# Attention with a routed expert layer: the gate work of the first six token pairs spread over nine steps

## The chip, the cores and the metric

The kernel runs on one core of a Trainium2 chip. The metric is the device time of one execution in microseconds (us); before the change it is 973.6 us, the median of three runs (972.81 to 974.79). The engines named below are PE (TensorE, matmuls and transposes), DVE (VectorE), ACT (ScalarE), POOL (GpSimd) and SP (SyncE, which issues DMAs here). PSUM is the memory that PE writes, SBUF the one that all engines share. A row of the timeline gives the start from the span's start, the duration, the engine, the source line, the operation and the tiles, out<-in.

## The reference

Three layers follow one another, on 4 x 576 = 2304 tokens of width 512:

```python
# 1. attention, 8 heads of 64, a causal window of 128 tokens, a bias that falls with distance
scores = scale * q @ k.T ; scores = where(mask, scores + bias, -1e9)
attn = exp(scores - max) ; attn /= sum + 1e-9 ; x = attn @ v
# 2. a routed layer: each token goes to its best two of 8 experts (512 -> 1024 -> 512)
noisy = x @ w_gate + log1p(exp(x @ w_noise)) * noise
top2 = the two largest ; w = softmax over them
out[token] += w * (relu(x[token] @ w1[e]) @ w2[e])
# 3. a dense layer for all tokens (512 -> 2048 -> 512)
out = (relu(x @ w_in) ** 2) @ w_out
```

## The kernel before

The order of the work on each engine is the order in which the program calls the functions; nothing reorders it. Tokens come in 18 tiles of 128 (`NT`), and attention runs in 36 steps (`NV`), two for each tile, four heads to a step. In step v, PE does the scores of step v + 2 (`s_step`, line 257), the transposes of the exponentials of step v + 1 (`t_step`, line 279) and the product with the values of step v (`pv_step`, line 303, called PV below). DVE reduces the scores in four instructions (line 262: add the bias, take the extreme), ACT takes the exponential (268) and copies the transposes out of PSUM (281), and DVE divides by the row sums (`norm`, 314 to 320). The finished tile is stored to `xd` by SP (326).

Beside this, each pair of tiles needs its routing: `gate_t` transposes a tile on PE (333) and ACT copies it (337); `gate_w` (344) and `gate_m` (352) are the two matmuls of the gate, `gate_o` 0 to 4 on DVE (363 to 377) finds the best two experts and makes their one-hot rows `oh`; `rank` (387) counts on PE, with matmuls against a triangle and ones, how many earlier tokens chose the same expert, and updates the running count `acc` (390); `place` 0 to 5 on DVE (397 to 422) turns this into a slot number `pos`; `scatter` on POOL (428) writes the token's number to that slot by two indirect DMAs for each tile. `gate_t`, `gate_w`, `gate_m` and `rank` all write to the one PSUM bank of tag "c".

Where this stands is set by a table: `at(v, slot, f, ...)` puts a call into a slot of step v, and `run(v, slot)` makes the calls of a slot. Slots 0 to 3 are on DVE behind each of the four score reductions, slot 4 stands between the transposes and PV, slot 5 at the step's end behind PV and `norm`:

```python
s_step(v + 2, v)          # slots 0 to 3 are run inside, behind the four reductions
t_step(v + 1)
run(v, 4)
pv_step(v); norm(...)     # and loads of q, k, v; the weight chunk of POOL (prep_one)
run(v, 5)
```

POOL also splits eight chunks of the expert weights in these steps (`prep_one`, line 108 a cast, line 110 a subtraction of 1024 columns), one each fourth step. Three blocks of the first expert's tokens are fetched while attention still runs: `early_table` (501, SP) loads the list of slots once the first 6, 10 or 14 tiles are scattered, `gather` (441, POOL, an indirect DMA) fetches the rows of that list, and `x_in` (448, PE) transposes them. After the last step the experts' matmuls follow, and then the dense layer.

Of the kernel before, what the change touches and what calls it, by code (L numbers as in the profile page):

```python
# [17 lines left out]
OP = mybir.AluOpType  # L18
# [11 lines left out]
PARTS = (6, 10, 14)  # L30
# [19 lines left out]
def attn_moe_ffn(ctx: ExitStack, tc: tile.TileContext, qt, kt, vt, wgn, noise, w1, w2, w_in, w_out,  # L50
                 consts, out):
    nc = tc.nc
# [18 lines left out]
    def bank(tag):  # L71
        if tag == "b":
            return psum.tile([128, 2, 512], F32, name="psb", tag="b", bufs=2)
        return psum.tile([128, 512], F32, name="ps" + tag, tag=tag, bufs={"a": 3, "c": 1}[tag])
# [11 lines left out]
    nload, nprep = [0], [0]  # L86
# [47 lines left out]
    acc = const.tile([128, 2, 8], BF16, name="acc")  # L134
# [17 lines left out]
    def load_q(i):  # L152
        Q[i] = qp.tile([128, 4, 128], F32, name="q", tag="q", bufs=4)
        nc.sync.dma_start(out=Q[i], in_=qt[i])

    def load_k(b, k0=0, k1=S):
        if b:
            K[b] = qp.tile([128, 4, S], F32, name="k", tag="k", bufs=2)
        nc.sync.dma_start(out=K[b][:, :, k0:k1], in_=kt[b][:, :, k0:k1])

    def load_v(n):
        b, p = divmod(n, 5)
        V[n] = qp.tile([128, 2, 8, 65], F32, name="v", tag="v", bufs=5)
        nc.sync.dma_start(out=V[n], in_=vt[b][:, 2 * p:2 * p + 2])
# [55 lines left out]
    P2, PT, PX, XI, G = {}, {}, {}, {}, {}  # L220
# [3 lines left out]
    def at(v, slot, f, *a):  # L224
        todo.setdefault((v, slot), []).append((f, a))

    def run(v, slot):
        for f, a in todo.pop((v, slot), []):
            f(*a)
# [42 lines left out]
    def t_step(v):  # L272
        PT[v] = []
        for j, p2 in enumerate(P2.pop(v)):
            flat = p2.rearrange("p a n -> p (a n)")
            ps = bank("a")[:, :384]
            for m in range(3):
                sl = slice(m * 128, (m + 1) * 128)
                nc.tensor.transpose(ps[:, sl], flat[:, sl], ident)
            pt = wk.tile([128, 3, 128], F32, name="pt", tag="pt", bufs=4)  # L280
            nc.scalar.activation(out=pt, in_=ps.rearrange("p (m c) -> p m c", m=3), func=AF.Copy)
            PT[v].append(pt)

    def pv_step(v):
        i, g = divmod(v, 2)
        px = bank("b")[:, :, :130].rearrange("p a (j d) -> p a j d", j=2)
        PX[i, g] = px
        mms = []
        for part in range(2):
            for j, pt in enumerate(PT[v]):  # L290
                for x in range(2):
                    b, t = divmod(2 * i + x, TB)
                    sl = slice(64 * x, 64 * x + 64)
                    for a in range(2):
                        h = 4 * g + 2 * j + a
                        if part == 0:
                            if a or t:
                                mms.append((x, a, j, pt[:, 2 * a, sl], vs(b, t - 1 + a)[:, h, :]))
                        elif a == 0 or t > 1:
                            r = slice(64 * a, 64 * a + 64)  # L300
                            mms.append((x, a, j, pt[r, 1, sl], vs(b, t - 2 if a else t + 1)[r, h, :]))
        for n, (x, a, j, l, r) in enumerate(mms):
            nc.tensor.matmul(px[64 * x:64 * x + 64, a, j, :], l, r,  # L303
                             start=not any(m[:2] == (x, a) for m in mms[:n]),
                             stop=not any(m[:3] == (x, a, j) for m in mms[n + 1:]), skip_group_check=True)
        del PT[v]
# [72 lines left out]
    def rank(p):  # L379
        oh = G["oh", p]  # L380
        rk = bank("c")[:, 0:16].rearrange("p (q w) -> p q w", q=2)
        G["rk", p] = rk
        for q in range(2):
            terms = [(tri, oh[:, q])] + [(ones, oh[:, 0])] * q + [(ones, acc)]
            for m, (l, r) in enumerate(terms):
                for k in range(2):
                    nc.tensor.matmul(rk[:, q, :], l, r[:, k, :], start=(m + k == 0),
                                     stop=(m + k == len(terms)))
        for q in range(2):
            nc.vector.tensor_tensor(out=acc, in0=acc, in1=oh[:, q], op=OP.add)  # L390

    def place(p, n):
        gs, oh = G["gs", p], G["oh", p]
# [120 lines left out]
    last = NV - 1  # L514
    for p in range(NT // 2):
        v = 4 * p + 3
        end = v == last
        at(v - end, 4, gate_t, 2 * p)
        at(v + 1, 4, gate_t, 2 * p + 1)
        at(v + 2, 0 if end else 4, gate_w, p)  # L520
        at(v + 2, 0 if end else 5, gate_m, p)
        o = v + 2 if end else v + 3
        for n, c in enumerate((0, 0, 0, 1, 2)):
            at(o, c, gate_o, p, n)
        at(o, 4 if end else 5, rank, p)
        for n, c in enumerate((0, 1, 1, 2, 2, 3)):
            at(o + 1, c, place, p, n)
        at(o + 1, 3, scatter, 2 * p)
        if end or 2 * p + 2 == PARTS[-1]:
            at(o + 1, 4, scatter, 2 * p + 1)  # L530
        else:
            at(o + 2, 3, scatter, 2 * p + 1)
    at(3, 3, more_consts)
    at(4, 4, zero_rows)
    for j, (v, w, x) in enumerate(((17, 18, 20), (25, 26, 28), (2 * PARTS[-1] + 3, 2 * PARTS[-1] + 4, last + 1))):
        at(v, 4, early_table, j)
        at(w, 5, gather, 0, j, True)
        at(x, 5, x_in, 0, j)
    at(last, 5, keep_warm, 24)
# [7 lines left out]
    def v_free(n):  # L547
        b, m = divmod(n, 5)
        return 9 * b + min(2 * m + 3, 8)
# [3 lines left out]
    for v in range(-2, NV + 3):  # L553
        s_step(v + 2, v)
        if 0 <= v + 1 < NV:
            t_step(v + 1)
        run(v, 4)
        if 0 <= v < NV:
            i, g = divmod(v, 2)
            pv_step(v)  # L560
            for n in range(3):
                norm(i, g, n)
            if g:
                if nq < NT:
                    load_q(nq)
                    nq += 1
                while nv < 5 * B and v_free(nv - 5) <= 2 * i + 1:
                    load_v(nv)
                    nv += 1
                if nk < B and 2 * i + 1 >= 9 * (nk - 1) + 1:  # L570
                    load_k(nk)
                    nk += 1
            if v % 4 == 2 and nprep[0] < 8:
                prep_one("pool", "pool")
        run(v, 5)

# [32 lines left out]
    for c in range(16):  # L609
        c = 8 * (c % 2) + c // 2  # L610
# [343 lines left out]
    last = E - 1  # L954
# [175 lines left out]
    end = 56 * NSB  # L1130
# [85 lines left out]
    for n, (s, u, kk) in enumerate(batches):  # L1216
# [8 lines left out]
        for k in range(2):  # L1225
            st, en = kk + k == 0, kk == 3 and k == 1
            for m, (p, o, lead) in enumerate(((P1, b13[:, 0:256], True), (P2, b26[:, 0:256], True),
# [9 lines left out]
                if m == 0:  # L1237
                    p1, u3 = tmp[2 + late_][:, 0:256], tmp[late_][:, 0:256]
                    x, y = [rows.tile([128, DM], F32, name="x", tag="r", bufs=6) for _ in range(2)]
# [71 lines left out]
```

## Time and profile before

| | |
|---|---|
| median of three runs | 973.6 us (972.81 to 974.79) |
| the profiled execution, and its span | 974.33 us, 972.6 us |
| PE busy | 956.8 us, 98% of the span |
| DVE, ACT, POOL busy | 69%, 48%, 41% |
| from 0 to 140 us: PE, DVE, ACT, POOL busy | 131.68, 98.93, 99.40, 66.63 us |
| from 140 us to the end: PE busy | 825.17 of 832 us |

Matmuls are pipelined and their ends are modelled, so a stretch of PE is best read from the start of one group to the start of the next. The "[idle <-X]" at the end of a row is idle time of that engine in front of the instruction, and what ended it. Idle time of an engine that is not the bottleneck costs nothing.

### The profile page before, as it was taken

The page shows a single profiled execution, that of the slowest core. Times are in us where ns is not written, and L with a number is a line of the kernel's source. Part 1 is how long each engine was busy: PE and PEld are TensorE (multiplying, and loading weights), DVE is VectorE, ACT ScalarE, POOL GpSimd, SP SyncE. Part 2 cuts the span into 40 slices and gives each one's busy share as a digit, 9 for nine tenths or more (in the row PEclk, how much of TensorE's full clock was granted, in tenths as well). Part 3 has the DMA queues.
Part 4 walks back from the last instruction along what each step waited for, and adds up shares of the span by engine and source line. Part 5 has one row for each costly group of instructions (what it writes and reads, how often), then busy time and mean ns, then how long its engine had stood idle before and what let it go on. Part 6 is the DMA issues. An engine that isn't in the chain of part 4 may idle for free. (4 is left out here: it accounts for less than half of the span.)

```text
span 972.6 us, 19636 instructions
## 1 busy us (share of the span) xinstructions
PE 956.8 (98%) x7438; PEld 878.9 (90%) x7438; DVE 668.2 (69%) x1452; ACT 463.2 (48%) x887; POOL 401.8 (41%) x433
## 2 busy tenths in 40 slices
PE   9999999999999999999999999999999999999997
PEld 6777789898998989899898898999999999999997
DVE  5777754657686776757774436778577899877773
ACT  7778733334343443433343346655555564434341
POOL 1565542124232333415334032624211624888880
PEclk9999999999999999999999999999999999999999
DMA  9767525456667576656655453966537874443331
GB/s 324 283 213 271 176 89 155 143 172 215 204 212 233 165 238 193 236 186 210 203 196 192 149 174 94 300 197 175 163 102 222 234 230 156 152 137 125 130 109 44
DMA packets 118199, 180.00 MB, mean 185 GB/s; under 512 B 11232, under 2 KB 66288, under 8 KB 117712
## 3 DMA queue, kind: packets, MB, share of 16 engines
q1 hardware_dynamic: 107120, 146.77, 46.8%
q0 software_dynamic: 10976, 31.90, 10.5%
q8 instruction: 59, 0.97, 0.4%
q14 instruction: 44, 0.36, 0.1%
HBM read 124.33 MB, written 54.30 MB: 184 GB/s over the span
## 5 line engine op out<-in xcount | busy, mean ns | idle before, releaser
L476 ACT ACTIVATE ha<-psa 128x384 fp32r<-128x384 f32 x64 | 31.3, 491 | 94.8 <-PE psa L472 93.2
L872 POOL TENSOR_TENSOR gs<-xb 128x256 f32<-128x256 f32 x62 | 60.2, 992 | 29.3 <-DVE wc L872 15.4
L268 ACT ACTIVATE p<-p,mx 128x192 f32<-128x192 f32 x144 | 57.5, 450 | 27.4 <-DVE mx L262 26.6
L689 POOL TENSOR_TENSOR et<-ex,et 128x512 f32<-128x512 f32 x16 | 20.9, 1304 | 111.5 <-DVE ex L685 111.5
L710 POOL DMA_INDIRECT yr<-yg,pos x36 | 37.3, 1037 | 68.6 <-DVE ha L477 45.1
L477 DVE SCALAR_TENSOR_TENSOR ha<-psa,ha 128x384 fp32r<-128x384 f32 x64 | 35.4, 553 | 42.6 <-ACT ha L476 37.5
L472 PE MATMUL psa<-xa,wa 128*128 128x384 f32 x288 | 55.0, 343 | 0.0
L428 POOL DMA_INDIRECT slots<-tok,pos x36 | 35.0, 972 | 45.7 <-DVE rs L314 30.0
L886 POOL DMA_DIRECT2D raw<-w x49 | 27.2, 561 | 63.5 <-DVE wb L872 18.4
L441 POOL DMA_INDIRECT xr<-xd,gidx x40 | 44.8, 1119 | 20.9 <-issue 6.1
L472 PE MATMUL psa<-xa,wc 128*128 128x384 f32 x288 | 53.3, 335 | 0.0
L791 PE MATMUL psb<-wa,ha 128*128 128x512 f32 x216 | 52.8, 396 | 0.0
L472 PEld LDWEIGHTS psa<-xa,wa 128*128 128x128 f32 x288 | 51.0, 194 | 0.2
L262 DVE CUSTOM_DVE_ANT_0 p<-psb,bias 128x192 f32<-128x192 f32 x144 | 45.8, 352 | 6.1 <-PE psb L257 5.4
L472 PEld LDWEIGHTS psa<-xa,wc 128*128 128x128 f32 x288 | 49.6, 188 | 0.2
L795 ACT ACTIVATE yo<-psb 128x512 f32<-128x512 f32 x38 | 22.7, 598 | 54.4 <-PE psb L791 38.7
L791 PEld LDWEIGHTS psb<-wa,ha 128*128 128x128 f32 x216 | 39.5, 188 | 7.8
L689 POOL TENSOR_TENSOR ex<-ex 128x512 f32<-128x512 f32 x12 | 15.6, 1302 | 74.6 <-DVE ex L685 74.6
L791 PE MATMUL psb<-wb,ha 128*128 128x512 f32 x176 | 46.3, 397 | 0.0
L110 DVE TENSOR_TENSOR wa<-raw,wa 128x1024 fp32r<-128x1024 f32 x20 | 25.7, 1284 | 29.4 <-ACT wa L106 29.3
L872 DVE TENSOR_TENSOR wc<-gs,wc 128x512 fp32r<-128x512 f32 x48 | 44.4, 965 | 0.4 <-ACT wc L872 0.4
L303 PEld LDWEIGHTS psb<-v,pt 64*64 64x64 f32 (+1 forms) x1056 | 32.8, 135 | 11.0 <-issue 7.7
(330 smaller groups left out, 2726.9 us busy)
## 6 DMA issues: line engine op xcount, KB each, us to landing
raw<-in_w_dram SPq DMA_DIRECT2D x64, 512.0 KB, 4.9
xb<-gmid SPq DMA_DIRECT2D x72, 256.0 KB, 2.9
v<-in_vt_dram SPq DMA_DIRECT2D x20, 520.0 KB, 5.3
yg<-yo SPq DMA_DIRECT2D x40, 256.0 KB, 3.1
raw<-w POOLq DMA_DIRECT2D x36, 256.0 KB, 3.8
gmid<-yo SPq DMA_DIRECT2D x48, 192.0 KB, 3.2
ex<-in_w_in_dram SPq DMA_DIRECT2D x16, 512.0 KB, 4.1
ex<-in_w_out_dram SPq DMA_DIRECT2D x16, 512.0 KB, 3.5
```

The lines of the kernel that those rows point to most:

```text
L262: nc.vector.tensor_tensor_reduce(out=p2[j][:, a, :], in0=ps[:, a, j, :], in1=bias[:, 4 * g + 2 * j + a, :], op0=OP.add, op1=OP.min, scale= ...
L268: nc.scalar.activation(out=p2[j][:, a, :], in_=p2[j][:, a, :], func=AF.Exp, bias=mx[j][:, a:a + 1], scale=-1.0)
L303: nc.tensor.matmul(px[64 * x:64 * x + 64, a, j, :], l, r, start=not any(m[:2] == (x, a) for m in mms[:n]), stop=not any(m[:3] == (x, a, j) ...
L428: st = nc.gpsimd.indirect_dma_start(out=slots, out_offset=bass.IndirectOffsetOnAxis(ap=pos[:, i, k:k + 1], axis=0), in_=tok[:, i:i + 1], i ...
L441: nc.gpsimd.indirect_dma_start(out=XR[e, j], out_offset=None, in_=xd[0:PARTS[j] * 128] if early else xd, in_offset=bass.IndirectOffsetOnAx ...
L472: nc.tensor.matmul(o, w[wp][:, f * 128:(f + 1) * 128], x[:, xp, d, :], start=(n == 0), stop=(n == 11))
L476: nc.scalar.activation(out=hi, in_=ps, func=AF.Relu)
L477: nc.vector.scalar_tensor_tensor(out=lo, in0=ps, scalar=0.0, in1=hi.bitcast(F32), op0=OP.max, op1=OP.subtract)
L689: nc.gpsimd.tensor_tensor(out=x, in0=af, in1=cf, op=OP.add)
L710: nc.gpsimd.indirect_dma_start(out=YR[i, k], out_offset=None, in_=yg, in_offset=bass.IndirectOffsetOnAxis(ap=pos[:, i, k:k + 1], axis=0))
L791: nc.tensor.matmul(py, h[:, hq], wc[wp][:, wsl], start=(f + n == 0), stop=(f == 7 and n == 2))
L872: f(**a)
```

## The change

The table for the pairs 0 to 5 (`2 * p + 2 < PARTS[-1]`) is rewritten; the pairs 6 to 8 keep theirs. With v = 4p + 3, pairs 0 to 4 now have: the two `gate_t` in slot 5 (they were in slot 4) of steps v and v + 1; `gate_w` in slot 4 of v + 2; `gate_m` in slot 4 of v + 3 (it was in slot 5 of v + 2); `gate_o` 0 to 2 in v + 4 and 3 to 4 in v + 5 (all five were in v + 3); `rank` and `place` 0 in slot 5 of v + 6; the update of `acc`, which becomes a function `count`, and `place` 1 to 5 in v + 7 (`place` was in v + 4); the first scatter in v + 7 and the second in v + 9 (they were in v + 4 and v + 5). Pair 5 has all of `gate_o` in v + 4, `rank` and `place` 0 in v + 5, the rest of `place` and the first scatter in v + 6, and the second scatter in v + 7. The early blocks move: tables from steps 17 and 25 to 21 and 28, gathers from 18 and 26 to 22 and 30, `x_in` from 20 and 28 to 24 and 32; the third stays. POOL's weight chunks move from steps 2, 6, 10, ... 30 to 2, 4, 8, 12, ... 28.

```diff
--- before.py
+++ after.py
@@ -386,8 +386,10 @@
                 for k in range(2):
                     nc.tensor.matmul(rk[:, q, :], l, r[:, k, :], start=(m + k == 0),
                                      stop=(m + k == len(terms)))
+
+    def count(p):
         for q in range(2):
-            nc.vector.tensor_tensor(out=acc, in0=acc, in1=oh[:, q], op=OP.add)
+            nc.vector.tensor_tensor(out=acc, in0=acc, in1=G["oh", p][:, q], op=OP.add)
 
     def place(p, n):
         gs, oh = G["gs", p], G["oh", p]
@@ -515,6 +517,26 @@
     for p in range(NT // 2):
         v = 4 * p + 3
         end = v == last
+        if 2 * p + 2 < PARTS[-1]:
+            mid = 2 * p + 4 >= PARTS[-1]
+            at(v, 5, gate_t, 2 * p)
+            at(v + 1, 5, gate_t, 2 * p + 1)
+            at(v + 2, 4, gate_w, p)
+            at(v + 3, 4, gate_m, p)
+            for n, c in enumerate((0, 0, 1, 2, 3) if mid else (0, 0, 1)):
+                at(v + 4, c, gate_o, p, n)
+            if not mid:
+                at(v + 5, 0, gate_o, p, 3)
+                at(v + 5, 1, gate_o, p, 4)
+            o = v + 5 if mid else v + 6
+            at(o, 5, rank, p)
+            at(o, 5, place, p, 0)
+            at(o + 1, 0, count, p)
+            for n, c in enumerate((0, 1, 1, 2, 3)):
+                at(o + 1, c, place, p, n + 1)
+            at(o + 1, 3, scatter, 2 * p)
+            at(o + 2 if mid else o + 3, 3, scatter, 2 * p + 1)
+            continue
         at(v - end, 4, gate_t, 2 * p)
         at(v + 1, 4, gate_t, 2 * p + 1)
         at(v + 2, 0 if end else 4, gate_w, p)
@@ -523,6 +545,7 @@
         for n, c in enumerate((0, 0, 0, 1, 2)):
             at(o, c, gate_o, p, n)
         at(o, 4 if end else 5, rank, p)
+        at(o, 4 if end else 5, count, p)
         for n, c in enumerate((0, 1, 1, 2, 2, 3)):
             at(o + 1, c, place, p, n)
         at(o + 1, 3, scatter, 2 * p)
@@ -532,8 +555,8 @@
             at(o + 2, 3, scatter, 2 * p + 1)
     at(3, 3, more_consts)
     at(4, 4, zero_rows)
-    for j, (v, w, x) in enumerate(((17, 18, 20), (25, 26, 28), (2 * PARTS[-1] + 3, 2 * PARTS[-1] + 4, last + 1))):
-        at(v, 4, early_table, j)
+    for j, (v, w, x) in enumerate(((21, 22, 24), (28, 30, 32), (2 * PARTS[-1] + 3, 2 * PARTS[-1] + 4, last + 1))):
+        at(v, 4 if j == 2 else 5, early_table, j)
         at(w, 5, gather, 0, j, True)
         at(x, 5, x_in, 0, j)
     at(last, 5, keep_warm, 24)
@@ -570,7 +593,7 @@
                 if nk < B and 2 * i + 1 >= 9 * (nk - 1) + 1:
                     load_k(nk)
                     nk += 1
-            if v % 4 == 2 and nprep[0] < 8:
+            if (v == 2 or v and v % 4 == 0) and nprep[0] < 8:
                 prep_one("pool", "pool")
         run(v, 5)
 
```

On PE, a step that ends with a gate transpose (line 333; 257 are scores, 279 transposes of the exponentials, 303 is PV) reads before, in step 19:

```order
L257 MATMUL psb<-k,q 64x192 x8
L279 MATMUL psa<-cst,p_1589 128x128 x3
L279 MATMUL psa<-cst,p_1595 128x128 x3
L333 MATMUL psc<-cst,xi 128x128 x4
L303 MATMUL psb<-v,pt 64x65 x16
```

The same gate transpose after the change, in step 23, with the place work's step 22 in front of it, which now holds the second gate matmul (352):

```order
L257 MATMUL psb<-k,q 64x192 x8
L279 MATMUL psa<-cst,p_1698 128x128 x3
L279 MATMUL psa<-cst,p_1704 128x128 x3
L352 MATMUL psc<-trs,gt 128x16 x2
L303 MATMUL psb<-v,pt 64x65 x16
L257 MATMUL psb<-k,q 64x192 x8
L279 MATMUL psa<-cst,p_1778 128x128 x3
L279 MATMUL psa<-cst,p_1784 128x128 x3
L303 MATMUL psb<-v,pt 64x65 x16
L333 MATMUL psc<-cst,xi 128x128 x4
```

The gate transpose went behind PV, and `gate_m` went between the transposes and PV of a step of its own.

On DVE, the update of the running count (line 390, after the change 392) and the cast that starts the place work (397, 399) stand before, for pair 3 in steps 18 and 19, so (262 is a score reduction, 320 the end of `norm`):

```order
L320 TENSOR_TENSOR xi<-psb,rs 128x256
L390 TENSOR_TENSOR acc<-acc,oh 128x16 x2
L262 ISA p_1589,mx<-psb,bias 128x192
L262 ISA mx 128x1
L397 CAST ri<-psc 128x16
L262 ISA p_1589,mx<-psb,bias 128x192
```

After the change, in steps 21 and 22:

```order
L320 TENSOR_TENSOR xi<-psb,rs 128x256
L399 CAST ri<-psc 128x16
L262 ISA p_1778,mx<-psb,bias 128x192
L262 ISA mx 128x1
L392 TENSOR_TENSOR acc<-acc,oh 128x16 x2
L403 TENSOR_SCALAR ri<-ri 128x16
```

The two additions went from ahead of the first score reduction to behind it, and the cast the other way.

On POOL, around the gather of the first early block (line 441, after the change 443; 428 and 430 are scatters), before:

```order
L108 CAST wb<-raw 128x1024
L110 TENSOR_TENSOR wb<-raw,wb 128x1024
L441 DMA xr<-xd,gidx_109 128x512
L427 MEMSET spacer 1x1
L428 DMA slots<-tok,pos 9728x1
```

And after:

```order
L108 CAST wb<-raw 128x1024
L110 TENSOR_TENSOR wb<-raw,wb 128x1024
L429 MEMSET spacer 1x1
L430 DMA slots<-tok,pos 9728x1
L429 MEMSET spacer 1x1
L430 DMA slots<-tok,pos 9728x1
L443 DMA xr<-xd,gidx_109 128x512
```

The first tile's two scatters of pair 3 went in front of the gather, which stood ahead of them.

## Rows read from the trace of the kernel before

**Rows 1.** Windows, steps 3-10, 11-22, 23-26, 27-32: stretch, length, busy us, clock, DMA share.

```profile
16.36:44.73 28.37, 26.13 (x495) 19.98 (x485) 21.02 (x126) 21.54 (x58) 15.73 (x17) 1.00 0.83 305
44.73:86.55 41.82, 40.36 (x723) 30.73 (x723) 31.69 (x202) 32.79 (x86) 23.81 (x31) 1.00 0.74 260
86.55:100.27 13.72, 13.22 (x247) 10.05 (x247) 10.47 (x66) 10.73 (x29) 7.58 (x9) 1.00 0.60 191
100.27:121.18 20.91, 20.43 (x355) 15.57 (x357) 15.93 (x100) 16.92 (x44) 11.20 (x17) 1.00 0.57 191
```

**Rows 2.** Waits from 8 to 130 us: who waited, for whom, total, times, longest.

```profile
PE psc L387 <- DVE oh L375: 3.1, 5, 1.2
```

**Rows 3.** PE timeline, steps 20 to 24: start, us, operation, tile, out<-in.

```profile
78.88 0.66 PE L448 MATMUL psa<-cst,xr 128*128 128x128 f32 x4
79.47 0.88 PE L257 MATMUL psb<-k,q 64*64 64x192 f32 x16
80.28 0.88 PE L279 MATMUL psa<-cst,p 128*128 128x128 f32 x6
81.08 0.64 PE L344 MATMUL psc<-xt,wg_sb 128*32 128x256 f32 x8
81.65 1.13 PE L303 MATMUL psb<-v,pt 128*64 128x65 f32 x32
82.71 0.62 PE L352 MATMUL psc<-trs,gt 128*128 128x16 f32 x4
83.26 0.88 PE L257 MATMUL psb<-k,q 64*64 64x192 f32 x16
...
86.11 0.20 PE L387 MATMUL psc<-oh,tri 128*128 128x8 bf16 x2
...
86.55 0.88 PE L257 MATMUL psb<-k,q 64*64 64x192 f32 x16
87.36 0.88 PE L279 MATMUL psa<-cst,p 128*128 128x128 f32 x6
88.08 0.63 PE L333 MATMUL psc<-cst,xi 128*128 128x128 f32 x4
88.64 1.13 PE L303 MATMUL psb<-v,pt 128*64 128x65 f32 x32
...
89.81 0.87 PE L257 MATMUL psb<-k,q 64*64 64x192 f32 x16
...
92.12 1.13 PE L303 MATMUL psb<-v,pt 128*64 128x65 f32 x32
93.07 0.33 PE L257 MATMUL psb<-k,q 64*64 64x192 f32 x2
```

**Rows 4.** PE timeline, the score group of step 16.

```profile
61.84 0.65 PE L257 MATMUL psb<-k,q 64*64 64x128 f32 x16
```

**Rows 5.** VectorE timeline, step 23.

```profile
87.06 0.36 DVE L390 TENSOR_TENSOR acc<-acc,oh 128x16 bf16<-128x16 bf16 x2
...
89.39 0.35 DVE L262 CUSTOM_DVE_ANT_0 p<-psb,bias 128x192 f32<-128x192 f32 x1
```

**Rows 6.** GpSimd timeline, step 6.

```profile
28.05 2.35 POOL L110 TENSOR_TENSOR wa<-raw,wa 128x1024 fp32r<-128x1024 f32 x1
```

**Rows 7.** VectorE timeline, step 6.

```profile
29.26 1.19 DVE L375 TENSOR_TENSOR oh<-iota,sel 128x32 bf16<-128x32 uint32 x1
```

**Rows 8.** GpSimd timeline, steps 24 and 25: first of four scatters, then the cast.

```profile
90.10 1.01 POOL L428 DMA_INDIRECT slots<-tok,pos  x1 [5.95 <-DVE rs L314]
...
94.93 1.05 POOL L108 CAST wb<-raw 128x1024 fp32r<-128x1024 f32 x1
```

**Rows 9.** Tile view of xr, all 40 gathers: issue to landing.

```profile
DMA to landing us min/median/max: 3.2/5.1/6.9
```

**Rows 10.** ScalarE timeline, step 20.

```profile
79.19 0.61 ACT L337 ACTIVATE xt<-psc 128x512 f32<-128x512 f32 x1
```

**Rows 11.** DMA view from 60 to 130 us: the table loads.

```profile
gidx<-slots SPq DMA_DIRECT2D x3, 0.5 KB, 2.0
```

## The prediction

> **What bounds the kernel now.** I read the engine table first: PE is busy 98% of the span, so a change counts where PE stands still or does dearer work. The code puts the change into steps 3 to 32 of the attention loop, so I cut that part by the windows view into four stretches whose borders are starts of a step's score group on PE: steps 3 to 10, 11 to 22, 23 to 26 and 27 to 32 [rows 1]. There PE works for 26.1 of 28.4, 40.4 of 41.8, 13.2 of 13.7 and 20.4 of 20.9 us, while VectorE, ScalarE and GpSimd have a fifth or more of their time free, and the granted clock is 1.00. So PE sets the pace and has little to give back. The waits view names its largest stall: the rank matmuls wait 3.1 us in five places for VectorE's one-hot rows [rows 2]. The PE timeline of steps 20 to 24 [rows 3] has the prices, read from start to start, because ends of matmuls are modelled: scores to transposes 0.81 (79.47 to 80.28); transposes to a group with another tile shape 0.80 (80.28 to 81.08), to gate transposes of their own shape 0.72 (87.36 to 88.08); gate transposes to PV 0.56, gate_w to PV 0.57; PV to scores 0.95 (92.12 to 93.07), but PV to a 128-wide group 1.06 (81.65 to 82.71); four transposes in front of scores 0.59 (78.88 to 79.47), gate_m 0.55, ranks 0.44.
>
> **The change, part by part.** One pair before costs four steps: 3.79 (gate_w and gate_m), 3.29 (ranks), 3.26 and 3.26 (gate transposes), 13.60 in all [rows 3].
>
> Gate transposes go from ahead of PV to behind it. PE pays 0.81 + 0.80 + 1.06 + 0.59 = 3.26, against 0.81 + 0.72 + 0.56 + 0.95 = 3.04: dearer by 0.22, twelve times. But before did not run at 3.04: the steps last 3.26, and the first because the next scores (89.81) need the fourth score reduction, started at 89.39 with the place work in between [rows 5]. So these steps stay at 3.26: a stall turns into PE work.
>
> Ranks join gate_w: 0.81 + 0.80 + 0.57 + 1.06 + 0.44 = 3.68, and the one-hot is a step old, so no wait for it. gate_m gets a step with count and places. PE needs only 0.81 + 0.72 + 0.56 + 0.95 = 3.04 there (gate_m to PV taken like gate transposes to PV), but VectorE does not: place work that made 3.26 now also has the two count additions between the reductions, where before they ran ahead of the first one, in idle time; two of 0.18 more [rows 5], one cast less, +0.2: 3.46. A pair: 3.26 + 3.26 + 3.68 + 3.46 = 13.66, as much as before without collisions.
>
> Collisions are what goes. While GpSimd subtracts a chunk (28.05, 2.35 us) [rows 6], VectorE's one-hot comparison at 29.26 takes 1.19 us instead of some 0.19, and ends as the subtraction ends [rows 7]. After the change a subtraction follows four scatters (4.83 from 90.10 to 94.93) and a cast of 1.05 [rows 8], so it starts 6 us behind the first scatter, which comes 0.3 after the following step's scores (90.10 after 89.81): in the gate_w step, where VectorE's gate work reads PSUM.
>
> Steps 3 to 10: two gate steps of 3.26, gate_w alone 0.81 + 0.80 + 0.57 + 0.95 = 3.13, gate_m alone 3.04, then a pair: 26.35 against 28.37, -2.0. The third chunk comes earlier, right behind the second one in GpSimd's order and as soon as its weights land, and its subtraction can hit the first pair's one-hot: between 0 and the 1.0 of rows 7; I take 0.5. Net -1.5.
>
> Steps 11 to 22: three pairs, 40.98, less 0.5 for two narrower score groups (0.65 busy [rows 4] against 0.88), which both kernels have: 40.5 against 41.8, -1.3. Of that 0.7 is a block transpose (0.59 + 0.11) that leaves for step 24.
>
> Steps 23 to 26: a pair, plus that transpose. Behind gate transposes, of its own shape, it costs 0.48 (four of the six that take 0.72): 14.14. Here I add a wait. Step 22 now holds place and scatter of the fourth pair, and on GpSimd two scatters stand in front of the first early gather. They start 0.3 into step 23, take 2.4, so the gather starts at 2.7 and lands 5.1 later [rows 9], at 7.8. PE reaches the transpose at 3.26 + 0.81 + 0.80 + 1.06 + 0.48 = 6.4: it waits 1.4. The scatter must also wait until the table load has read the slots. SP issues that behind a store and two loads of step 21, I estimate 2 us into step 22, and it lands 2.0 later [rows 11], some 0.6 behind the places: wait 2.0, between 0 (gather at its shortest, 3.2, and the table in time) and 4.7 (gather at 6.9, table 1.5 late). Behind it on PE is the whole attention, so it counts in full. 16.1 against 13.7, +2.4.
>
> Steps 27 to 32: the sixth pair is squeezed. Step 27 has all one-hot work, like before's 3.29. In step 28 gate transposes and ranks share the one PSUM bank of that tag, so the ranks wait for ScalarE's copy. In step 20 that copy ended at 79.19 + 0.61 = 79.80 [rows 10], 0.92 after PE was through with PV (78.88): the step costs 0.81 + 0.72 + 0.56 + 1.06 + 0.95 + 0.44 = 4.54, and 4.6 with a little wait of the transposes too; bounds 3.6 (copy early) and 5.0. Then 3.79, 3.29, 3.26 and 3.26 + 0.70 for the second block transpose, now in step 32: 22.2. Its gather stands behind four scatters, starts 4.9 into step 30, lands at 10.0; PE is there at 3.29 + 3.26 + 0.81 + 0.72 + 0.56 + 1.06 = 9.7: 0.3 more (0 to 2.1). 22.5 against 20.9, +1.6.
>
> SP's weight loads, moved with GpSimd's chunks, I cost at nothing: each has four steps until it is used, the load between the first two chunks excepted, which GpSimd waits for in any case. The last three pairs keep their places, and the tail behind attention is PE's, so a shift passes through.
>
> **Sum:** -1.5 - 1.3 + 2.4 + 1.6 = +1.2 us. The profiled execution took 974.33 us (span 972.6), so 975.5 for it; the median of the runs, 973.6, lies 0.7 lower, and on it I forecast 974.8.
>
> **A rule weighed against the rows.** Rows 6 and 7 show a subtraction holding a comparison of two SBUF operands; no such VectorE instruction met GpSimd's cast. The Trainium skill, "SBUF — State Buffer", Who interferes with whom, says that a VectorE instruction with two SBUF inputs contends with any GpSimd instruction that reads SBUF, and that the later one blocks wholly. By that the cast would block too, which no row here shows.
>
> **Rivals.**
> 1. Forecast: the stall of the ranks is paid back by waits for the early gathers and the squeezed pair: 974.8 (own range 973.2 to 975.5).
> 2. Slower: the first early block. If gathers land in 6 us and the table 1.5 late, the first wait is 2.7 + 1.5 + 6.0 - 6.4 = 3.8 and the second 4.9 + 6.0 - 9.7 = 1.2, 2.7 over mine: 977.5. It decides once the first wait is over 2.8. For it: the landings go up to 6.9 [rows 9]. Against: DMA share there is only 0.6 [rows 1].
> 3. Faster: gathers land in 3.2, no wait at all (-2.3), and the third chunk hits nothing (-0.5): 972.0; without the wait for ScalarE in step 28 (-0.95) 971.1. For it: DMA is less busy in the later steps.
> 4. The cast blocks as well: in steps 7 and 8 the third chunk then holds VectorE up to 1.05 longer [rows 8]: 975.8. This is the rule above.
> 5. The change doesn't do what it says: the subtractions drift onto other two-operand work, count or places. Two or three hits of 0.3 to 1.0 cost 1.5: 976.3.
>
> **How the numbers follow.** 0.2% is 1.95 us, about what a measurement of this kernel can tell from no change. Chances: forecast 0.45; rival 2 0.25; rival 3 0.15; rival 4 0.07; rival 5 0.08. Rivals 2, 4 and most of 5 are slower (0.38), rival 3 faster (0.15), the rest within 0.2% (0.47). The range goes from rival 3 at 972.0 to rival 2, 977.4.
>
> **What would show it.** Right: no rank wait for one-hot rows in steps 9 to 25; no VectorE instruction of 0.3 us or more among the small gate ones; gate transpose steps at 3.26, the place steps at 3.4 to 3.5 with scores released by the reduction; PE waiting some 2 us for the DMA of the first early block, and about 1 us for ScalarE in front of the sixth ranks. Wrong: no wait for the block in step 24 (then it is faster), place steps at 3.1, or gate steps over 3.4.

## The result: slower by one per cent

The median after the change is 984.12 us (982.37 to 986.67, 6 runs), against 973.94 us (972.81 to 975.07, 6 runs) before: ratio 1.0100, 95% interval 1.0084 to 1.0115. The forecast, 974.8 us, was wrong, and its range ended at 977.4. The profiled execution took 982.96 us (span 981.1), 8.5 us of span more than before. Two executions of one kernel below (the early block alone: 1150 and 1548 us, at a mean clock of 0.76 and 0.56) were slow ones and are left out of its numbers.

The windows view of the changed kernel, cut at the same score groups as [rows 1] (stretch, length, busy time of PE, PEld, DVE, ACT and POOL with counts, granted clock, DMA share, GB/s):

```profile
17.18:43.49 26.31, 25.64 (x484) 19.62 (x475) 19.42 (x115) 20.84 (x56) 11.49 (x9) 1.00 0.91 340
43.49:86.01 42.52, 39.52 (x719) 30.29 (x719) 33.79 (x201) 32.36 (x85) 22.84 (x30) 1.00 0.73 251
86.01:107.96 21.95, 15.90 (x250) 11.76 (x250) 10.92 (x67) 11.49 (x30) 8.61 (x11) 0.84 0.39 133
107.96:131.61 23.65, 20.81 (x363) 15.89 (x363) 17.07 (x113) 18.12 (x47) 15.04 (x24) 1.00 0.44 145
```

Against [rows 1] that is -2.06, +0.70, +8.23 and +2.74, in sum +9.61. One stretch carries the loss, and its granted clock is 0.84 where the others have 1.00. The attention loop also begins 0.82 later; behind it the kernel is some 1.9 us shorter, mostly because a stretch at the lower clock when the expert work begins, which the profile of before has, is absent in this one.

The waits from 8 to 140 us (who waited, for whom: total, times, longest) answer [rows 2]:

```profile
PE psa L450 <- DMA xr<-xd,gidx: 6.2, 2, 5.8
PE psb L257 <- DVE rs L314: 2.7, 6, 0.6
PE psc L387 <- ACT xt L337: 1.1, 1, 1.1
...
PE psc L387 <- DVE oh L375: 0.2, 1, 0.2
```

The ranks' wait for one-hot rows, 3.1 us before, is gone as predicted; the 0.2 left belongs to a later pair. In its place stands the wait for the first early block, 5.8 us. The PE timeline at that place:

```profile
91.94 0.66 PE L333 MATMUL psc<-cst,xi 128*128 128x128 f32 x4
98.36 1.12 PE L450 MATMUL psa<-cst,xr 128*128 128x128 f32 x4 [5.77 <-DMA xr<-xd,gidx]
99.41 0.42 PE L246 MATMUL psb<-far,ones 64*64 64x256 bf16 x2
99.42 1.54 PE L257 MATMUL psb<-k,q 64*64 64x192 f32 x16
100.89 1.54 PE L279 MATMUL psa<-cst,p 128*128 128x128 f32 x6
```

The same score and transpose groups took 0.87 us each at 89.28 and 90.08. The windows of 2 us say why: the clock is granted at 0.50 (1.2 GHz) when PE resumes.

```profile
94.00:96.00 2.00, 0.00 (x0) 0.00 (x0) 0.00 (x0) 0.00 (x0) 1.78 (x4) 1.00 1.04 396
96.00:98.00 2.00, 0.00 (x0) 0.00 (x0) 0.00 (x0) 0.00 (x0) 1.91 (x2) 0.54 0.22 78
98.00:100.00 2.00, 1.64 (x18) 1.31 (x20) 0.00 (x0) 0.48 (x1) 1.10 (x2) 0.50 0.00 0
100.00:102.00 2.00, 2.00 (x17) 1.41 (x12) 1.65 (x8) 0.68 (x3) 0.00 (x0) 0.50 0.00 0
102.00:104.00 2.00, 2.00 (x33) 0.95 (x34) 0.66 (x3) 1.68 (x5) 0.00 (x0) 0.75 0.00 0
```

Where the block's lateness comes from is read on three engines. On SP (start, duration of the issue), the table load stands behind a store and two loads of step 21:

```profile
83.02 0.34 SPq L326 DMA_DIRECT2D xd<-xi  x1
83.45 1.31 SPq L154 DMA_DIRECT2D q<-in_qt_dram  x1
84.86 0.38 SPq L164 DMA_DIRECT2D v<-in_vt_dram  x1
85.34 0.37 SPq L503 DMA_DIRECT2D gidx<-slots  x1
```

VectorE has the fourth pair's places at 85.94:

```profile
85.78 0.16 DVE L424 TENSOR_TENSOR pos<-gs,cst 128x4 int32<-128x4 f32 x1
```

but GpSimd starts the first scatter only at 89.44, 4.1 us after the table load's issue, because the scatter may not write the slots before the table has been read. The releaser that the view infers (DVE rs) had long been done; that it was the load is shown by the run below that moves the load alone (there the scatter starts at 86.40).

```profile
89.44 0.99 POOL L430 DMA_INDIRECT slots<-tok,pos  x1 [9.11 <-DVE rs L317]
...
92.03 1.00 POOL L443 DMA_INDIRECT xr<-xd,gidx  x1 [0.30 <-issue]
```

The gather stands behind both scatters, and its landing took 6.3 us, with the 16 DMA engines full until 96 us (above, a share of 1.04 in 94 to 96, 0.22 in the next 2 us):

```profile
DMA to landing us min/median/max: 6.3/6.3/6.3
```

In steps 11 to 22 the steps with the second gate transposes took 3.72, 3.52 and 3.72 us. GpSimd and VectorE in the first of them (rows of the kind of [rows 6] and [rows 7]):

```profile
48.59 1.05 POOL L108 CAST wa<-raw 128x1024 fp32r<-128x1024 f32 x1
```

```profile
48.53 1.16 DVE L375 TENSOR_TENSOR oh<-iota,sel 128x32 bf16<-128x32 uint32 x1
```

The comparison, some 0.19 us by itself, ends as the cast ends (49.64). The cast blocks it, not the subtraction, and does so in the third and fourth pair too (1.27 and 1.16 us). In the first pair it is the third chunk's subtraction, which runs from 33.16 to 35.53, that holds the comparison:

```profile
34.61 0.96 DVE L375 TENSOR_TENSOR oh<-iota,sel 128x32 bf16<-128x32 uint32 x1
```

### The profile page after: what moved, and what is told of

It reads as the page before. It is cut to its first block, busy times and chain, and to the rows that moved or that the text cites. A ratio compares the mean times of both kernels' runs of the same rounds, so it can differ in the third digit from the quotient of the medians.

```text
span 981.1 us, 19631 instructions
## 1 busy us (share of the span) xinstructions
PE 956.6 (97%) x7438; PEld 878.5 (90%) x7438; DVE 669.0 (68%) x1452; ACT 463.2 (47%) x887; POOL 399.9 (41%) x433
## 5 line engine op out<-in xcount | busy, mean ns | idle before, releaser
L818 ACT ACTIVATE yo<-psb 128x512 f32<-128x512 f32 x38 | 22.7, 597 | 54.5 <-PE psb L814 40.5
```

## The experiments

Each kernel ran against the kernel before on the same chip (medians there 974.9, 974.3 and 974.5 us). First all of them by stretches, in us, from their profiled executions with the borders of [rows 1]; then the ratio of the times to before.

| kernel | 3-10 | 11-22 | 23-26 | 27-32 | sum | median us | ratio, 95% |
|---|---|---|---|---|---|---|---|
| before | 28.37 | 41.82 | 13.72 | 20.91 | 104.82 | 973.9 | 1 |
| predicted | 26.85 | 40.5 | 16.1 | 22.5 | 105.95 | 974.8 | |
| changed | 26.31 | 42.52 | 21.95 | 23.65 | 114.43 | 984.1 | 1.0084 to 1.0115 |
| block's transposes in step 27 | 26.29 | 42.52 | 14.90 | 25.78 | 109.49 | 980.3 | 1.0039 to 1.0088 |
| table load ahead | 26.17 | 42.56 | 14.11 | 23.23 | 106.07 | 976.7 | 1.0007 to 1.0037 |
| table and gather ahead | 26.46 | 42.56 | 14.94 | 23.33 | 107.29 | 976.7 | 1.0011 to 1.0040 |
| wait filled | 26.46 | 42.55 | 20.00 | 23.82 | 112.83 | 983.4 | 1.0076 to 1.0117 |
| early block alone | 28.75 | 41.36 | 18.68 | 21.00 | 109.79 | 978.7 | 1.0029 to 1.0065 |
| chunks alone | 28.65 | 42.95 | 13.71 | 20.79 | 106.10 | 977.9 | 1.0018 to 1.0047 |
| table ahead, chunks back | 25.93 | 42.15 | 20.44 | 27.57 | 116.09 | 987.8 | 1.0118 to 1.0151 |
| table ahead, one-hot later | 25.93 | 40.57 | 14.33 | 23.88 | 104.71 | 979.2 | 1.0034 to 1.0064 |
| table ahead, sixth ranks | 27.28 | 42.52 | 17.42 | 25.95 | 113.17 | 977.4 | 1.0015 to 1.0041 |
| table ahead, three edits | 25.65 | 39.75 | 18.38 | 23.10 | 106.88 | 977.7 | 1.0015 to 1.0056 |
| three edits, both blocks ahead | 25.65 | 39.76 | 13.65 | 21.99 | 101.05 | 970.6 | 0.9944 to 0.9975 |
| before, chunk between scatters | 27.03 | 42.83 | 15.24 | 20.82 | 105.92 | 974.2 | 0.9982 to 1.0006 |

**The block's transposes moved from step 24 to 27**

```diff
-((21, 22, 24), (28, 30, 32), ...)   # table load, gather, transposes
+((21, 22, 27), (28, 30, 32), ...)
```

> Only the transposes of the first early block move, from step 24 to step 27; its table load, its gather, the scatters and all gate work stay as in the changed kernel. Theory A (the block's wait and the fall of the granted clock behind it are the loss): PE has three more steps, over 10 us, so the wait of 5.77 us is gone, the granted clock stays at 1.00, and the groups at half clock (L450 1.06, scores to transposes 1.47, transposes to gate_w 1.47, gate_w 0.86, together some 2.1 us more than at full clock) are gone too: 984.1 - 5.8 - 2.1 = 976.2 us. Theory B (the spread gate work itself costs, the wait only stands where another stall would): 982 to 984 us, with the idle time on other groups of steps 23 to 28.

Measured 980.33 us: the wait for the block is gone, but of the loss in the median only a little over a third (half of it in the stretches). What takes its place is read in step 26. The late table still makes the scatters late, so GpSimd's chunk comes later too, and its subtraction (95.95 to 98.30) meets VectorE's count additions, 1.57 us for two that take 0.36 in [rows 5]:

```profile
95.95 2.35 POOL L110 TENSOR_TENSOR wb<-raw,wb 128x1024 fp32r<-128x1024 f32 x1
```

```profile
96.96 1.57 DVE L392 TENSOR_TENSOR acc<-acc,oh 128x16 bf16<-128x16 bf16 x2
```

PE then waits 1.75 us for a score reduction, and in step 28 the ranks wait 1.33; windows of 4 us behind the two, from 102 and from 110 us, have a clock of 0.67 and 0.68. So the wait for the block can be taken away and other waits come in its place: the cause lies further back.

**The table load ahead of the store and loads of step 21**

```diff
-at(v, 4 if j == 2 else 5, early_table, j)
+at(v, 5 if j == 1 else 4, early_table, j)
```

> Only the issue of the first early block's table load moves, from behind the store and the two loads of step 21 to ahead of them. Theory A with the table load as the cause of the long wait: the table lands some 2.0 us after its issue, the fourth pair's first scatter starts at its pos (85.9 to 86.2) and not at 89.44, the gather is issued 3.2 us earlier, and the wait falls from 5.77 to 1.4 to 2.5 us; with a shorter idle stretch the clock falls less or not at all: 978 to 981 us. If the gather's landing alone were late (rival: DMA is busy with the loads behind), the scatters start early but the wait stays above 4 us: 982 to 984 us.

Measured 976.66 us, 7.5 below the changed kernel, better than the 978 to 981 expected. The load was issued at 82.34 and landed 2.3 us later (its row in SP's timeline, and in the DMA view, which gives the time to landing last):

```profile
82.34 0.33 SPq L503 DMA_DIRECT2D gidx<-slots  x1
```

```profile
gidx<-slots SPq DMA_DIRECT2D x1, 0.5 KB, 2.3
```

The places came at 86.12, the scatter started at 86.40, the gather at 89.00:

```profile
86.40 0.99 POOL L430 DMA_INDIRECT slots<-tok,pos  x1 [5.87 <-DVE rs L317]
...
89.00 1.00 POOL L443 DMA_INDIRECT xr<-xd,gidx  x1 [0.30 <-issue]
```

The gather landed in 3.7 us in this profile, and PE waited for nothing:

```profile
92.79 0.66 PE L450 MATMUL psa<-cst,xr 128*128 128x128 f32 x4
```

One DMA of 0.5 KB, moved past 1 MB of others, is worth three quarters of the loss.

**Table load and gather both ahead of the fourth pair's scatters**

```diff
-((21, 22, 24), ...)
+((20, 21, 24), ...)     # and the load in slot 4
```

> The first block's table load goes to step 20 and its gather to step 21, ahead of the fourth pair's scatters in GpSimd's order; its transposes stay in step 24. Theory A: the gather has over 10 us, no wait in step 24, the clock stays at 1.00: 984.1 - 7.9 = 976.2 us, the same as with the transposes moved. Theory B: 982 to 984 us.

Measured 976.69 us, as expected for theory A to half a microsecond; the xr wait is 0.3. There is no difference from the run before, so from the load's place on, GpSimd's order costs nothing in the median. In its profile the cast held the one-hot in step 24 (1.08 us), and the ranks of the next step waited 0.95.

**The wait filled with 96 unread matmuls**

```diff
 def x_in(e, j):
+    if (e, j) == (0, 0):
+        ps = bank("a")[:, 0:128]
+        for _ in range(96):
+            nc.tensor.matmul(ps, tri, ones, start=True, stop=True)
```

> The changed kernel with 96 more bf16 matmuls (128x128) on PE in front of the first early block's transposes, in a PSUM bank of their own; nothing reads them. In the changed kernel 24 such matmuls took 1.3 us, so these take some 5.3 us and lie inside the wait of 5.77. They add nothing to the result. If the fall of the granted clock behind the wait is what idle time on PE brings, and costs 2.1 us, the clock stays at 1.00 in 96 to 104 us and the time is 982.0 us. If the fall costs nothing or comes from something else, 984 us.

```profile
91.96 5.52 PE L464 MATMUL psa<-ones,tri 128*128 128x128 bf16 x96
98.06 0.63 PE L450 MATMUL psa<-cst,xr 128*128 128x128 f32 x4 [0.57 <-DMA xr<-xd,gidx]
98.62 0.87 PE L257 MATMUL psb<-k,q 64*64 64x192 f32 x16
```

The unread matmuls end at 97.48, and PE waits only 0.57 us. The granted clock is 1.00 throughout 92 to 108, and the block transposes are back at 0.63, the scores at 0.87. Steps 24 and 25 take 13.40 us against 15.36, so the clock's part is the 2.0 us expected, in the profiles. The medians differ by only 0.7 (983.4 against 984.1), and their intervals overlap: in the time it is not shown.

**The early block's move alone, in the kernel before**

```diff
-((17, 18, 20), (25, 26, 28), ...)   # load in slot 4
+((21, 22, 24), (28, 30, 32), ...)   # load in slot 5, but the third
```

> Only the early blocks' move, in the kernel before: table loads in slot 5 of steps 21 and 28, gathers in steps 22 and 30, transposes in steps 24 and 32. The table load is as late as in the changed kernel (issued behind the store and both loads, landing some 4 us after its own issue), and the first gather waits for it, but no pair's scatters stand between: the gather starts some 4 us into step 22 or 23 and lands 5 to 6 us later, near the time when PE comes to the transposes of step 24. Theory (the late table needs the scatters of the fourth pair to become a wait of 5.8 us): wait 0 to 2.5 us, ratio 1.000 to 1.003. Rival (the late position alone costs what it cost in the changed kernel): wait over 4 us and ratio 1.006 or more.

Measured ratio 1.0047: between the two theories, above the 1.003 of mine. No scatter stands in front of the gather here, yet it starts only at 92.26, 4.6 us behind the table load's issue (87.62), as the scatter did in the changed kernel; that it waited for the load is inferred from that, for the releaser named had long been done:

```profile
92.26 1.00 POOL L441 DMA_INDIRECT xr<-xd,gidx  x1 [6.44 <-PE psb L257]
```

```profile
97.35 0.66 PE L448 MATMUL psa<-cst,xr 128*128 128x128 f32 x4 [2.91 <-DMA xr<-xd,gidx]
```

The window behind has a clock of 0.61. So the move of the early blocks alone costs half of the loss. (The load itself went out here 1.65 us after the loads ahead of it, whose last issue ended at 85.97.) How the rest divides between the scatters that stand between it and the gather, and the longer fall of the clock, no run tells.

**The chunk move alone, in the kernel before**

```diff
-if v % 4 == 2 and nprep[0] < 8:
+if (v == 2 or v and v % 4 == 0) and nprep[0] < 8:
```

> Only the chunk move, in the kernel before. There both scatter calls of a pair already stand ahead of the chunk, so its cast starts when they end, whichever step it is emitted in; only the third chunk comes earlier. Theory (moving the chunks alone does nothing): ratio 0.999 to 1.001, the subtractions still end in the one-hot steps, and the ranks' waits stay near 3 us. Rival (the weight load that goes with each chunk moves with it and makes it late or early): ratio beyond 0.998 or 1.002.

My theory missed: 977.94 us, ratio 1.0032. The casts do start when the scatters end, as before. But the weight load that a chunk issues on SP now goes out in step 16, at 65.23, while the third pair's scatters land, and the early table's load, by my reading of one profile, waits for these:

```profile
65.23 0.38 SPq L93 DMA_DIRECT2D raw<-in_w_dram  x1
71.47 0.33 SPq L501 DMA_DIRECT2D gidx<-slots  x1
```

From the last scatter's end to the table load it is 3.5 us (68.01 to 71.47), in the kernel before 1.6 (66.84 to 68.42), where the weights load comes later. The gather starts 2.85 us later and PE waits 0.93 in step 20, where it waited for nothing [rows 3]. In step 6 the ranks wait 2.0 us for the held comparison (1.2 in the kernel before), but the early block alone, which has the old chunk order, shows 2.0 there too, so that is not the chunk move's.

**Table load ahead, chunks where before had them**

```diff
-if (v == 2 or v and v % 4 == 0) and nprep[0] < 8:
+if v % 4 == 2 and nprep[0] < 8:
```

> The version with the early table's load (976.7 us) and GpSimd's chunks put back to where the kernel before has them in program order (after steps 2, 6, 10 and so on, between the two scatter calls of a pair), the rest as changed. Cast and subtraction then come 2.4 us earlier, the subtraction in the second gate-transpose step, where VectorE has its one-hot comparison: if the moved chunks are worth what the prediction said, the comparison is held by the subtraction (up to 2.3 us) and steps 11 to 22 become slower than 42.5 us by 1 to 2: 978. If the place of the chunk makes no difference: 976.7.

Measured 987.79 us, 11 above the base, for another reason than expected: steps 11 to 22 are no slower (42.15). Program order now has the chunk between the scatters and the early gather, and the gather waits for cast and subtraction:

```profile
87.02 0.97 POOL L430 DMA_INDIRECT slots<-tok,pos  x1 [0.21 <-issue]
88.00 1.05 POOL L108 CAST wb<-raw 128x1024 fp32r<-128x1024 f32 x1
89.13 2.36 POOL L110 TENSOR_TENSOR wb<-raw,wb 128x1024 fp32r<-128x1024 f32 x1
91.65 1.01 POOL L443 DMA_INDIRECT xr<-xd,gidx  x1 [0.16 <-issue]
```

PE waits 3.9 us for the first block and 3.7 for the second, each with a fall of the clock (0.50 in 96 to 100). In steps 11 to 22 the subtraction holds the comparison about as long (1.07 us) as the cast did.

**The one-hot behind the fourth reduction** (on the table-load version, as the next two)

```diff
-at(v + 5, 1, gate_o, p, 4)
+at(v + 5, 3, gate_o, p, 4)
```

> The changed kernel with the first early table's load ahead of the store and loads of step 21 (the version that ran at 976.7 us), and with VectorE's one-hot comparison (L375) emitted behind the fourth score reduction of its step, not behind the second: by then GpSimd's cast is over. If the cast holds the comparison, and that is why the second gate-transpose steps took 3.72 us and not 3.26: those steps come to 3.3, the comparison to 0.2 us from 1.16, and with three or four such pairs the time to 975.0 to 975.4. If the long step has another cause (PE's dearer order, the reductions), the steps stay at 3.7 and the time at 976.7.

In the profile it does what was expected: the steps of 3.72, 3.52 and 3.72 take 3.26, 3.07 and 3.26, and steps 11 to 22 take 40.57, the forecast's 40.5. The comparison is still held until the cast ends (48.76), but starts behind the reductions that PE waits for:

```profile
47.71 1.05 POOL L108 CAST wa<-raw 128x1024 fp32r<-128x1024 f32 x1
```

```profile
48.20 0.62 DVE L375 TENSOR_TENSOR oh<-iota,sel 128x32 bf16<-128x32 uint32 x1
```

The median does not show it: 979.24 us, above the base, with runs from 973.3 (the profiled one) to 981.7. The slower runs have a lower mean clock (0.994 to 0.995 against 1.000), which would fit PE standing still somewhere in them; no profile of one exists, so where is left open. The run below that fetches both blocks ahead bears on it.

**The sixth pair's ranks ahead of PV**

```diff
-at(o, 5, rank, p); at(o, 5, place, p, 0)
+at(o, 4 if mid else 5, rank, p); at(o, 4 if mid else 5, place, p, 0)
-at(v + 1, 4, gate_t, 2 * p + 1)                    # seventh pair
+at(v + 1, 5 if 2 * p == PARTS[-1] - 2 else 4, gate_t, 2 * p + 1)
```

> The same base (976.7 us) with one knot of the sixth pair undone: in step 28 its ranks run ahead of PV, as soon as step 28 begins, and the gate transposes that shared their PSUM bank go behind PV. If the ranks' wait of 1.06 us for ScalarE's copy is what makes that step 4.6 us, it falls to some 3.7, and the next one, whose gate_w followed at once, changes by less than 0.3 either way: 975.8 us. If ScalarE is the bound there, the wait moves to gate_w of step 29: 976.7.

The step fell from 4.63 to 3.53 us, and the next rose from 4.35 to 4.63: -0.8, as expected. The median, 977.43, hides it, for the profiled run (983.64) waits again for the two blocks:

```profile
PE psa L450 <- DMA xr<-xd,gidx: 5.4, 2, 3.5
```

**All three edits** (the third: count behind the norm)

```diff
-at(o + 1, 0, count, p)
+at(o + 1, 5, count, p)
```

> Both edits of the other two runs, and the count additions moved from between the reductions of the place step to behind the norm of that step, where VectorE waits for the next scores. If all three hold: 3.55 to 3.65 us of the place steps become 3.3 to 3.4 (six pairs, 1.2 us in all), with 1.5 for the one-hot and 0.9 for the ranks: 973.1 us, a shade under the kernel before. If VectorE's order does not set the place steps: 974.3. If the gains only move the waits: 976.

Place steps fell from 3.54 to 3.65 us to 3.26 to 3.37, and steps 11 to 22 to 39.75, about as expected; the time, 977.72, did not follow. A faster PE comes to the blocks earlier, and waits 4.2 us for them, 3.0 at one. In two of these three versions, then, the profile shows the gain in the steps given back where the early gathers land; PE's wait for the blocks is none, 1.0, 5.4 and 4.2 us in the four profiles with only the table load ahead.

**Both early blocks ahead of the next pair's scatters, with the three edits**

```diff
-((21, 22, 24), (28, 30, 32), ...)
+((20, 21, 24), (28, 29, 32), ...)    # loads in slot 4, second gather in slot 2
```

> The changed kernel with the three edits of the run before (one-hot behind the fourth reduction, sixth pair's ranks ahead of PV, count behind the norm) and with both early blocks fetched earlier: the first table's load in step 20 and its gather in step 21, the second's in steps 28 and 29, each ahead of the next pair's scatters in GpSimd's order; the transposes stay in steps 24 and 32. If the waits for the two blocks are what made the times of the last versions spread over 8 us: no PE wait over 0.5 us for xr, steps 24 and 25 at 3.9 and 3.4 us, step 32 at 3.9, steps 3 to 32 in some 101 us against 104.8 in the kernel before, time 971 us (ratio 0.996 to 0.998). If the loss is in the spread gate work itself: ratio at least 1.002.

Measured 970.57 us (969.31 to 973.72), ratio 0.996, interval 0.9944 to 0.9975: faster than both kernels, and close to what was expected in every term: steps 24 and 25 at 3.69 and 3.63 (3.9 and 3.4), step 32 at 3.92 (3.9), steps 3 to 32 at 101.05 (101). No wait for xr is left in the view, and the windows have PE busy nearly throughout:

```profile
16.67:42.32 25.65, 25.48 (x483) 19.59 (x475) 18.50 (x113) 20.81 (x56) 11.48 (x9) 1.00 0.92 347
42.32:82.08 39.76, 39.09 (x718) 30.18 (x719) 32.13 (x201) 32.38 (x85) 22.81 (x29) 1.00 0.76 258
82.08:95.73 13.65, 13.63 (x250) 10.61 (x251) 10.75 (x67) 11.25 (x30) 8.66 (x12) 1.00 0.79 261
95.73:117.72 21.99, 20.71 (x363) 15.87 (x363) 17.04 (x115) 17.86 (x47) 14.53 (x22) 1.00 0.47 152
```

The only edits between this kernel and the one of 977.72 are the two earlier fetches, so these are worth 7 us in the time. Theory B (the spread gate work itself is the loss) falls with it, since the work is still spread over as many steps, though three of its calls stand in other slots than in the changed kernel. Without the three edits no version of the changed kernel was faster than before (the best, with the table load ahead, is 0.2% slower); the two fetches without them were not run.

**The kernel before with its chunk between the two scatter calls**

```diff
-if v % 4 == 2 and nprep[0] < 8:
+if v % 4 == 3 and nprep[0] < 8:   # early blocks (18, 18, 24), (26, 26, 32), loads in slot 5
```

> The kernel before, gate work untouched (four steps a pair), with GpSimd's chunk put between the two scatter calls of a pair and not behind both, so that its cast and subtraction come 2.4 us earlier; the early blocks' gathers and transposes a step or more later so that they need not wait. Theory (the collisions of GpSimd's subtraction with VectorE's gate work are what the change wins back in steps 3 to 22): the comparison never takes over 0.3 us, the ranks' waits fall from 3.1 us in all to some 2, and the time falls by 1 to 2 us against before, to a ratio of 0.998 to 0.999. Rival (the ranks wait for the chain gate_m, exp, max, one-hot within one step, whatever GpSimd does): ratio 1.000, with waits of 0.5 to 0.6 us left in every pair.

Measured ratio 0.9994, interval 0.9982 to 1.0006: the rival's value, but the profile does not bear out the rival's reason. No comparison is held any more (0.19 us at most), and five of the six ranks' waits are 0.22 to 0.28 us, less than either theory had. The sixth is 2.23, in step 22. There a subtraction holds another VectorE instruction with two SBUF operands, the gate's product with the noise (line 363, 0.17 by itself):

```profile
81.91 2.35 POOL L110 TENSOR_TENSOR wb<-raw,wb 128x1024 fp32r<-128x1024 f32 x1
```

```profile
82.10 2.18 DVE L363 TENSOR_TENSOR gs<-gs,nz_sb 128x16 f32<-128x16 f32 x1
```

Behind it the clock falls (0.89 in steps 23 to 26). So steps 3 to 10 gained 1.3 us, and steps 11 to 26 gave back 2.5. The kernel before has this kind of collision too: in four of its five places of ranks' wait (0.31 to 0.56 us) it is the product that ends with a subtraction, here in step 18, where the subtraction ends at 70.33; [rows 7] is the fifth.

```profile
69.91 0.45 DVE L363 TENSOR_TENSOR gs<-gs,nz_sb 128x16 f32<-128x16 f32 x1
```

With 0.22 to 0.28 left where nothing is held, I estimate that collisions made some 1.9 of the 3.1 us of [rows 2] (3.1 less five times 0.24). What moving GpSimd's work alone is worth, without a new collision elsewhere, no run tells.

## Why the prediction was wrong

The mechanism of the loss was in it, as a wait of 2.0 us and as rival 2; its size was not. Point by point:

- **Steps 23 to 26, the failed step:** "SP issues that behind a store and two loads of step 21, I estimate 2 us into step 22, and it lands 2.0 later", hence a wait of 2.0, bounded at 4.7. Measured 5.77. The load came 3.0 us into step 22 (one of the issues in front took 1.31 on SP), and the scatter started 4.1 behind it, not 2.0. [Rows 11] are landings of loads that stood ahead of the store and loads, and the change takes the load from that place; I carried the duration over. So the gather started 6.0 us into step 23, not 3.3 (+2.7); it landed in 6.3, not 5.1 (+1.2), inside [rows 9] but at their upper end, with the DMA engines full for most of it. PE was there 6.6 us into the step, predicted 6.4. The table load alone, put back ahead, gives 7.5 us of the 10.
- **The clock:** the sum priced the wait at its length. PE's idle stretch brought the granted clock to 0.50, and the groups behind cost 2 us more, which vanish in the profile when the wait is filled (the medians differ by 0.7). The profile of before has such a fall further on; I did not look for it there.
- **Steps 11 to 22:** 42.52 against 40.5. The sum placed only the subtraction, and found it harmless; the cast in front of it meets the comparison, in the second gate-transpose step of each pair. Rival 4 had the mechanism, but only for steps 7 and 8, at 0.07. The contention weighed there, of the Trainium skill ("SBUF — State Buffer", Who interferes with whom), is seen here: in the second to fourth pair the comparison takes 1.16, 1.27 and 1.16 us, where it takes 0.19 alone, and ends with the cast. That the later one waits does not come out of the records: these comparisons start 0.06 to 0.16 us before the casts, and the casts keep their 1.05. With the comparison moved the stretch takes 40.57.
- **Steps 27 to 32:** 23.65 against 22.5. The ranks' wait of 1.06 (predicted 0.95) and the second block's of 0.46 (0.3) are as forecast; the rest is mostly 0.5 of gate_m waiting for VectorE's copy in step 29, not in the sum.
- **Weight loads "at nothing":** wrong where the early table's load is near. Alone, the chunk move costs 3 us in the time; its profile shows a wait of 0.93 for the early block, and the rest is not placed.
- **Collisions:** "Collisions are what goes" holds for some 1.9 us of the ranks' wait of 3.1, though the comparison of rows 6 and 7 was one place of five and the noise product the other four. But new ones came with the new order, in the first to fourth pair's comparisons.
- **Right:** first gate steps 3.26; rank steps 3.67 (3.68); the one-hot wait gone. Steps 3 to 10 took 26.31, where the forecast was 26.85 with 0.5 for a hit by the third chunk. The hit came (0.96 us at 34.61) but cost PE only some 0.2, and step 6 took 2.85 instead of 3.04; that the stretch is so near the 26.35 of the sum without a hit is in part luck. Place steps were 3.54 to 3.65, not 3.46, and the count additions in them were the reason: moved, the steps take 3.26 to 3.37.
- **Chances:** 0.25 for rival 2 was low, and its price was bounded by the landings of the old order. 0.15 and 0.47 for faster and same rested on that.

## What to carry to other kernels

When a change moves a small transfer, look at what stands ahead of it on its issuing engine at the new place, and who may not go on until it has landed; a landing time belongs to a place in a queue, not to a transfer. Price a long wait on PE with the lower clock that follows it (here 2.0 us behind 5.8), and take the highest landing, not the median, where the DMA engines are full. When stalls are removed from one place, first fetch earlier what the faster engine will ask for next: here the spread gate work was 1.0% slower with late fetches, and 0.4% faster with early ones and three of its calls moved as well. And when an engine's work is moved off one collision, look for the next two-operand instruction that it meets at the new place.

## What the runs showed of the hardware

- A 0.5 KB load issued behind 256 and 520 KB loads held its successors for 4.1 us; ahead of them it landed in 1.5 to 3.6 (four profiles). The second block's table load landed in 4.6 to 6.5 us behind such loads (four profiles), and still in 5.5 where it was fetched earlier.
- GpSimd's cast holds VectorE's comparison of two SBUF operands until it ends (1.16 to 1.27 us for 0.19; 0.61 to 0.73 when the comparison starts later), as its subtraction does (1.19 in the kernel before). The subtraction does the same to the count additions (1.57 for 0.36) and to the noise product (2.18 for 0.17).
- PE stood without work for 5.8 us, and its granted clock fell to 0.50 (1.2 GHz) meanwhile; the windows from 98 to 102 have 0.50, the one from 102 to 104 has 0.75. With bf16 matmuls in the gap it stayed at 1.00.
- The 40 gathers of a run, of the same size, landed in 3.2 to 7.9 us; the first early one took 6.3 us in the changed kernel and 3.7 with the table load ahead.
